# Another order of loads, products and conversions in an attention and two-MoE kernel

## The chip, the cores and the metric

The kernel runs on one core of a Trainium2 chip. The metric is device time in microseconds (us) of one execution; lower is better. A core has five engines with a queue of instructions each: TensorE (PE in the rows; its weight loads are PEld), VectorE (DVE), ScalarE (ACT), GpSimd (POOL) and SyncE (SP). SP issues most transfers; 16 DMA engines carry them. A row that names an engine with a q (SPq, PEldq) is about its sequencer.

## The reference

```python
def reference(**kwargs):
    attn_out = _attn_ref(q, k, v, f)             # b=4, h=8, s=576, d=64
    x = attn_out.transpose(0, 2, 1, 3).reshape(2304, 512)
    x = _moe_ref(x, w_in, w_out)
    return _moe2_ref(x, w_gate, w_output_gate, w1, w2)

def _attn_ref(q, k, v, f):
    cum = np.cumsum(np.log(np.clip(f, 0.0001, 1.0)), axis=-1)
    scores = q @ k.T / sqrt(64) + cum[:, None] - cum[None, :]   # causal, then softmax, then @ v

def _moe_ref(x, w_in, w_out):                    # (2304, 512), w_in (512, 2048), w_out (2048, 512)
    h = x @ w_in
    return (h * np.clip(h + 3.0, 0.0, 6.0) / 6.0) @ w_out

def _moe2_ref(x, w_gate, w_output_gate, w1, w2): # 8 experts, w1 (512, 1024), w2 (1024, 512) each
    e_idx = np.argmax(x @ w_gate, axis=1)        # one expert per token, softmax weight gate_w
    out[mask] = gate_w[mask, None] * eom[mask, e, None] * (np.maximum(x[mask] @ w1[e], 0.0) @ w2[e])
```

Here eom is a sigmoid of x @ w_output_gate. w_in and w_out are float64, the other inputs float32. The kernel splits each operand into a float16 part and a bfloat16 rest and forms each product as three products of the parts.

## The kernel before, in words

**Attention.** Tokens of a batch come in pieces: q and k of piece 0 to 3 (four heads by 256 positions) and 4 (the last 64 positions), v in blocks of 128. `load` issues a piece's loads on SP; `prep` splits a piece into its parts (`split_kq`: ScalarE, then GpSimd) and turns it by a transposing transfer of SP (tiles K and q); pieces 0 and 1 of batch 0 are turned by TensorE instead. `prep_v` splits a block of v. A unit is a head with one or two blocks of rows. `score` gives it its products (L349) and VectorE's reduce with the mask (L394), `soft` ScalarE's exponentials, `turn` or a transposing transfer the turned probabilities, `pv` the products with v. The list `plan` says in which order units ("q", "t") and preparations ("p", "v") come; `attn_seq` walks it. The first 16 units (`first_units`, batch 0) run before any chunk.

**First MoE.** Its 2304 tokens are cut into six chunks of 384. The first half of a chunk has 16 groups of 12 products 128x384 (L840, tile mm); ScalarE and VectorE make g of them (L848 to L855). The second half has 4 groups of 48 products (L867), which ScalarE and VectorE evict into x (L876, L877). A chunk is 32 parts, and between parts attention units are put in, as many as `goals` and the pace (PACE, and PACE_END from chunk 4 on) ask for: the units of a chunk are to be through by that share of its parts. w_in and w_out come raw (512-KB loads, tiles wo and raw), and VectorE and ScalarE make float32 of their bits (L793 to L809) at the steps that PRE_CONV and CONV_AT list.

**Gate and second MoE.** When attention is through, `open_weights` reuses its memory for the experts' weights: a ring of three 512-KB buffers (stw) that SP loads, ScalarE converts (L1040) and VectorE gives the rest of (L1043); one such step is put in at every second part of a chunk. `gate_steps` picks a token's expert and rank. `gather` fetches an expert's tokens by an indirect transfer of GpSimd and turns them by one of SP, `expert1` and `expert2` hold the two products (L1152, L1171), and GpSimd scatters the rows to the output (L1178). Tokens beyond 384 of an expert would take further rounds, behind an If on `more` at the end; a block beyond an expert's count stands in an If of its own. The counts are loaded into registers of every engine (L1409).

TensorE, ScalarE and VectorE take their work in the written order, and SP and GpSimd too in the start.

Of the kernel before, what the change touches and what calls it, by code (L numbers as in the profile page):

```python
# [23 lines left out]

ATTN_FIRST = 200

PACE, PACE_END = 0.82, 0.75

PRE_CONV = (1, 3, 5, 7, 9, 11, 13, 15, 17, 19, 21, 22, 28, 29, 29, 30)

CONV_AT = (3, 4, 5, 7, 9, 11, 12, 14, 16, 17, 19, 20, 22, 24, 25, 27)

# [26 lines left out]
def attention_moe_kernel(ctx: ExitStack, tc: tile.TileContext, q, k, v, f, w_in, w_out,  # L59
# [316 lines left out]
    def score(u):  # L376
        kind, b = u[0], u[1]
        if kind == "q":
            h, qbs = u[2], u[3]
            N = sum(QW[x] for x in qbs)  # L380
            ms = ap1.tile([P, 576], F32, tag="ms", name="ms", bufs=3)
            nm = ap1.tile([P, 4], F32, tag="nm", name="nm", bufs=4)
            offs, off = [], 0
            sc = ps_sc.tile([P, 512], F32, tag="sc", name="sc")
            for qb in qbs:
                l1, l2 = q_cols(b, h, qb)
                w = QW[qb]
                scores(sc[:, off:off + w], h, qb, l1, l2)
                off += w
            off = 0  # L390
            for i, qb in enumerate(qbs):
                w = QW[qb]
                ps = sc[:, off:off + w]
                nc.vector.tensor_tensor_reduce(  # L394
                    out=pairs(ms[:, off:off + w]), in0=ps[:, 0:w].rearrange("p (c j) -> p c j", c=2),
                    in1=pairs(mask[:, 640 - w:640]), scale=-1.0 / PSC, scalar=3e38, op0=ALU.add, op1=ALU.min,
                    accum_out=nm[:, i:i + 1])
                tick()
                offs.append((off, w, i))
                off += w  # L400
            st[u] = [ms, nm, offs, N]
        else:
            h = u[2] * 2
            N = 576
            ms = ap1.tile([P, 576], F32, tag="ms", name="ms", bufs=3)
            nm = ap1.tile([P, 4], F32, tag="nm", name="nm", bufs=4)
            for j, (c0, w) in enumerate(((0, 512), (512, 64))):
                ps = ps_sc.tile([P, 512], F32, tag="sc", name="sc")
                for e in range(2):
                    po = slice(e * 64, e * 64 + 64)  # L410
                    l1, l2 = q_cols(b, h + e, 4)
# [12 lines left out]
                tick()  # L424
            st[u] = [ms, nm, [(0, 576, 1)], N]
# [188 lines left out]
    for b in range(B):  # L614
# [3 lines left out]
        for hp in range(H // 2):  # L618
            gb += [("q", b, 2 * hp, (3,)), ("q", b, 2 * hp + 1, (3,)), ("t", b, hp)]
        if b == 0:  # L620
            plan += ga[0:2] + [("p", 0, 2)] + ga[2:5] + [("p", 0, 3), ga[5], ("v", 0, 2)] + ga[6:]
            ends.append(len(plan) - 1)
            plan += gc[0:3] + [("p", 0, 4)] + gc[3:6] + [("v", 0, 3)] + gc[6:] + [None, gb[0], None, gb[1], ("v", 0, 4)]
            ends.append(len(plan) - 1)
# [37 lines left out]
    def attn_seq():  # L662
# [36 lines left out]
        for i in range(2):  # L699
            load(i, "kq")  # L700
        load(0, "v")
        setup()
        store_decay(cp)
        for hh in range(2):
# [7 lines left out]
            behind.pop(0)()  # L712
        load_next(nc.scalar)
        load_next(nc.scalar)
        load(2, "kqv")
        yield "end"
        prep_v(0, 0)
        yield "end"
        prep_v(0, 1)
        yield "end"  # L720
        load(3, "kq")
        for it in plan:
# [273 lines left out]

    ring, made, fetches = [], [], []

    def weights_steps(wp):

        parts, tiles = [], {}

# [31 lines left out]
        for i, (_, e, which, js) in enumerate(parts):  # L1034
            if (e, which) not in tiles:
                tiles[e, which] = (wp.tile([P, 2, KD, F2], F16, tag="W1", name="W1", bufs=2) if which == 0 else
                                   wp.tile([P, 2, F2 // P, DM], F16, tag="W2", name="W2", bufs=2))
# [79 lines left out]
    def gather(e, blocks, into=None):  # L1117
# [5 lines left out]
        else:  # L1123
            xs, xg = into[0], [into[1]]
        for j, s in enumerate(blocks):
            nc.gpsimd.indirect_dma_start(out=xg[j], out_offset=None,  # L1126
                                         in_=rows[0:NT if into is None else NBL * P, :],
                                         in_offset=bass.IndirectOffsetOnAxis(ap=slot[s][0][:, e:e + 1], axis=0))
            nc.sync.dma_start_transpose(out=xs[:, :, j * P:(j + 1) * P], in_=xg[j])
            xs_t[e, s] = (xs, j * P)  # L1130

    def h_tile(e, blocks, into=None):
        if into is None:
            n = F2 // P * 2 * NSB * P
            into = wof[:, e % 2 * n:(e % 2 + 1) * n].rearrange("p (a c b) -> p a c b", c=2, b=NSB * P)
        for j, s in enumerate(blocks):
            h_t[e, s] = (into, j * P)

# [117 lines left out]
    def pre_step():  # L1256
# [3 lines left out]
        for _ in range(PRE_CONV.count(nsteps[0])):  # L1260
            convert()
        for _ in range(1 + ready):
            if loads and (loads[0][0] == "wi" or ready):
                load_next(nc.sync)

    with tc.manual_schedule(engines={mybir.EngineType.SP, mybir.EngineType.Pool}):
        while len(complete) < need[0]:
            pre_step()
        for _ in range(LEAD):
            pre_step()  # L1270
    gate.append(gate[-1])
    held = False
    EARLY_CONV_DONE = 2 * NF - len(conv)
    assert len(conv) == len(CONV_AT), (len(conv), nsteps)
    goals = [due[need[c + 1] - 1] for c in range(NCH - 1)]
    mp2 = None
    px_ctx = ctx.enter_context(ExitStack())
    iota = None
# [123 lines left out]
        fetches[0]()  # L1402
    for g_ in first:
        run(g_, F2 // P)
    for e in range(2):
        for _ in expert2(e, ps_mm, (0,), wi[:, 1, e, 0:2 * DM].bitcast(F32)):
            pass
        if e == 0:
            regs.extend(nc.values_load(cnt[0:1, x:x + 1], min_val=0, max_val=NT) for x in range(E))  # L1409
            more = nc.values_load(nrounds[0:1, 0:1], min_val=0, max_val=NT // CAP)  # L1410

    def round_(first):

# [11 lines left out]
        blocks = main  # L1425
        if not first:
            blocks = [(0, 1)] * E
            wg = weights_steps(wp)
# [16 lines left out]
    round_(True)  # L1445
    manual.close()
    with tc.If(more > 0):
        RA = wi.rearrange("p a b c -> p (a b c)")[:, 0:NB * CAP].rearrange("p (n s) -> p n s", s=CAP)
        with tc.For_i(0, more, 1):
            nc.vector.tensor_scalar(out=rank, in0=rank, scalar1=-float(CAP), scalar2=None, op0=ALU.add)  # L1450
            for i in range(NB):
                rank_onehot(RA, i, 0, CAP)
            table(RA, 0, mp2, ps_mm, range(NSB), NB)
            round_(False)


# [28 lines left out]
```

## Time and profile before

| | us |
|---|---|
| median of 3 runs (lowest, highest) | 830.68 (830.33, 832.77) |
| the profiled execution | 827.96 |
| its span, first to last instruction | 826.2 |
| TensorE busy in it | 731.0 (88%) |
| VectorE, ScalarE, GpSimd busy | 453.1, 454.8, 316.7 |

Each execution's time includes what lies around the span. The granted clock is TensorE's, as a share of 2.4 GHz; 0.50 is 1.2 GHz. Its mean over the span is 0.943. A wait is shown in square brackets behind an instruction: how long its engine stood idle ahead of it, and what came last before it started.

### The profile page before, as it was taken

How to read it: one execution, taken by the hardware profiler on the slowest of the kernel's cores; microseconds unless marked ns; L12 is line 12 of the kernel's file. 1: busy time of each engine (PE TensorE's matmuls, PEld its weight loads, DVE VectorE, ACT ScalarE, POOL GpSimd, SP SyncE). 2: the span in 40 equal slices, each digit the busy share in tenths (PEclk: the TensorE clock that was granted, in tenths of full speed). 3: DMA queues.
4: the chain of work that ended last, by engine and by line, in shares of the span. 5: the costliest groups of instructions: out<-in, count | busy, mean ns of one | idle time of the engine just before them, and what ended most of it. 6: DMA issues, size and time to landing. Idle time of an engine off the chain costs nothing. (4 is left out here: it accounts for less than half of the span.)

```text
span 826.2 us, 16592 instructions
## 1 busy us (share of the span) xinstructions
PE 731.0 (88%) x6153; PEld 477.5 (58%) x6153; DVE 453.1 (55%) x1254; ACT 454.8 (55%) x904; POOL 316.7 (38%) x402
## 2 busy tenths in 40 slices
PE   4366888699999989999799999889998999999994
PEld 2254455456566656666466566446676766756761
DVE  7587786556852574278434855683142565536420
ACT  4575678666874677278755772562022565545420
POOL 7485557584554434155543451000032222320010
PEclk7576998989999999999899999999999999999997
DMA  6996869986678646386765564863087789969100
GB/s 158 276 227 148 190 130 192 212 196 150 95 161 157 135 90 122 54 178 129 158 112 123 86 94 126 269 200 102 1 173 135 202 269 298 305 196 267 66 37 28
DMA packets 268066, 129.00 MB, mean 156 GB/s; under 512 B 218946, under 2 KB 251810, under 8 KB 267972
## 3 DMA queue, kind: packets, MB, share of 16 engines
q1 hardware_dynamic: 255620, 104.71, 59.0%
q0 software_dynamic: 4960, 15.73, 5.3%
q10 hardware_dynamic: 7392, 7.34, 2.9%
q8 instruction: 54, 0.88, 0.5%
q14 instruction: 40, 0.33, 0.1%
HBM read 71.52 MB, written 10.08 MB: 99 GB/s over the span
## 5 line engine op out<-in xcount | busy, mean ns | idle before, releaser
L867 PE MATMUL mm<-g,wo 128*128 128x384 f16 (+1 forms) x1152 | 197.5, 330 | 0.0
L840 PE MATMUL mm<-xT,wi 128*128 128x384 f16 x912 | 165.9, 338 | 7.3 <-DVE g L855 4.5
L840 PEld LDWEIGHTS <-wi 128*128 128x128 f16 (+1 forms) x1152 | 112.3, 100 | 83.3 <-issue 19.6
L867 PEld LDWEIGHTS <-wo 128*128 128x128 f16 (+1 forms) x1152 | 111.6, 99 | 71.9 <-issue 3.7
L465 POOL TENSOR_TENSOR pn<-ms,pn 128x384 bf16<-128x384 f32 (+1 forms) x80 | 80.9, 1013 | 85.9 <-ACT pn L464 53.7
L1152 PEld LDWEIGHTS <-W 128*128 128x128 f16 (+1 forms) x1344 | 99.9, 98 | 12.6 <-issue 4.2
L1152 PE MATMUL mm<-g,W 128*128 128x256 f16 (+3 forms) x1152 | 97.3, 246 | 3.3 <-issue 1.9
L1171 PE MATMUL mm<-W,wo 128*128 128x512 f16 (+1 forms) x432 | 94.5, 379 | 0.6 <-PEq L1436 0.5
L456 ACT ACTIVATE ms<-ms,nm 128x512 f32<-128x512 f32 (+3 forms) x144 | 80.3, 577 | 10.4 <-DVE nm L394 7.6
L1043 DVE TENSOR_TENSOR W<-stw,W 128x1024 bf16<-128x1024 f32 x46 | 55.7, 1223 | 52.4 <-ACT W L1040 51.6
L394 DVE CUSTOM_DVE_ANT_1 ms<-sc,mask 128x128 f32<-128x128 f32 (+3 forms) x128 | 60.6, 486 | 31.4 <-PE sc L349 25.5
L1171 PEld LDWEIGHTS <-wo 128*128 128x128 f16 (+1 forms) x432 | 41.8, 98 | 50.7 <-ACT W L1040 1.2
L1178 POOL DMA_INDIRECT out_dram<-wo,ids x18 | 20.6, 1145 | 124.3 <-ACT wo L1177 102.3
L877 DVE SCALAR_TENSOR_TENSOR x<-mm,x 128x384 bf16<-128x384 f32 x24 | 13.4, 557 | 98.5 <-ACT x L876 98.5
L876 ACT ACTIVATE x<-mm 128x384 f16<-128x384 f32 x24 | 11.7, 489 | 87.7 <-PE mm L867 86.9
L1156 DVE SCALAR_TENSOR_TENSOR wo<-mm,wo 128x128 bf16<-128x128 f32 (+1 forms) x96 | 33.0, 355 | 47.5 <-ACT wo L1155 44.1
L349 PE MATMUL sc<-K,q 128*128 128x128 f16 (+2 forms) x192 | 49.0, 312 | 10.7 <-DVE nm L394 5.7
L349 PE MATMUL sc<-K,Q 67*128 67x128 f16 (+2 forms) x192 | 48.7, 310 | 9.4 <-DMA K<-cumd 3.5
L848 ACT ACTIVATE hr<-mm,bias 128x384 f32<-128x384 f32 x76 | 43.7, 575 | 24.2 <-PE mm L840 24.0
L1040 ACT ACTIVATE W<-stw 128x1024 f16<-128x1024 f32 x46 | 47.7, 1050 | 16.7 <-DMA stw<-in_moe_w_dram 16.5
L849 DVE SCALAR_TENSOR_TENSOR mm<-hr,mm 128x384 f32<-128x384 f32 x76 | 42.4, 558 | 25.7 <-ACT hr L848 25.3
L501 PE MATMUL pv<-vt,pt 128*128 128x65 f16 x320 | 41.3, 198 | 17.1 <-ACT pt L450 11.0
(216 smaller groups left out, 1254.5 us busy)
## 6 DMA issues: line engine op xcount, KB each, us to landing
stw<-in_moe_w_dram SPq DMA_DIRECT2D x46, 512.0 KB
stx<-in_moe_w_dram SPq DMA_DIRECT2D x18, 512.0 KB
wo<-in_moe_w_in_dram SPq DMA_DIRECT2D x14, 512.0 KB
raw<-in_moe_w_out_dram ACTq DMA_DIRECT2D x10, 512.0 KB
rows<-rw POOLq DMA_DIRECT2D x15, 256.0 KB
ld<-in_v_dram SPq DMA_DIRECT2D x13, 256.0 KB
ld<-in_k_dram SPq DMA_DIRECT2D x12, 256.0 KB
ld<-in_q_dram SPq DMA_DIRECT2D x12, 256.0 KB
```

What stands on the lines that cost most here:

```text
L349: nc.tensor.matmul(po, lhsT=lhs[0:rows], rhs=r if n > 1 else r[:, :, 0], start=x == 0, stop=x == 1)
L394: nc.vector.tensor_tensor_reduce(out=pairs(ms[:, off:off + w]), in0=ps[:, 0:w].rearrange("p (c j) -> p c j", c=2), in1=pairs(mask[:, 640 - ...
L456: nc.scalar.activation(out=ms[:, off:off + w], in_=ms[:, off:off + w], func=AF.Exp, scale=-1.0, bias=nm[:, i:i + 1])
L465: nc.gpsimd.tensor_tensor(out=lo.bitcast(BF16), in0=ms[:, 0:N], in1=hi, op=ALU.subtract)
L840: nc.tensor.matmul(ps[:, 0:w], lhsT=l.bitcast(BF16) if a else l, rhs=r.bitcast(BF16) if b2 else r, start=i == 0, stop=i == 3 * KD - 1)
L848: nc.scalar.activation(out=hr, in_=pw, func=AF.Relu, bias=bias3)
L849: nc.vector.scalar_tensor_tensor(out=pw, in0=hr, scalar=6.0, in1=pw, op0=ALU.min, op1=ALU.mult)
L867: nc.tensor.matmul(ps[:, 0:w], lhsT=l.bitcast(BF16) if a else l, rhs=r.bitcast(BF16) if b2 else r, start=i == 0, stop=i == 3 * NF - 1)
L1040: nc.scalar.activation(out=hi, in_=sts[i], func=AF.Copy)
L1043: nc.vector.tensor_tensor(out=lo.bitcast(BF16), in0=st, in1=hi, op=ALU.subtract)
L1152: nc.tensor.matmul(ps[:, 0:w], lhsT=l.bitcast(BF16) if a else l, rhs=r.bitcast(BF16) if b2 else r, start=i == 0, stop=i == 3 * KD - 1)
L1171: nc.tensor.matmul(ps, lhsT=l.bitcast(BF16) if a else l, rhs=r.bitcast(BF16) if b2 else r, start=i == 0, stop=i == 3 * NF2 - 1)
```

## The change

Seven things are changed.

1. k and q of piece 2 are loaded right behind v's first block, and `prep(0, 2)` stands ahead of the first units; `plan` loses that step, and the last four entries of PRE_CONV come down by one.
2. `pre_step` issues a w_in load only when its conversion is due within RAW_AHEAD steps.
3. `fill` gives TensorE 10 products 128x128 of constant tiles into unused columns behind each first unit's scores, and 24 at the end of the start. Nobody reads them.
4. `goals` are raised by AHEAD in chunks 1 to 3, and PACE_END falls from 0.75 to 0.42.
5. Register loads of the counts: two at first, then one after each expert.
6. The seventh to the twelfth gather are issued behind the sixth.
7. The last block of the last expert comes behind the If of the further rounds, which gets memory of its own.

```diff
-PACE, PACE_END = 0.82, 0.75
-PRE_CONV = (1, 3, 5, 7, 9, 11, 13, 15, 17, 19, 21, 22, 28, 29, 29, 30)
+PACE, PACE_END = 0.82, 0.42
+PRE_CONV = (1, 3, 5, 7, 9, 11, 13, 15, 17, 19, 21, 22, 27, 28, 28, 29)
+AHEAD = (0, 3, 9, 9, 0)
+RAW_AHEAD = 7
+FILL, LAST_FILL = 10, 24
...
+    def fill(ps, n):
+        for _ in range(n):
+            nc.tensor.matmul(ps[:, 384:512], lhsT=minus, rhs=mask[:, 0:P], start=True, stop=True,
+                             skip_group_check=True)
...
+            if first_units(u):
+                fill(sc, FILL)
...
-            plan += ga[0:2] + [("p", 0, 2)] + ga[2:5] + [("p", 0, 3), ga[5], ("v", 0, 2)] + ga[6:]
+            plan += ga[0:2] + [("v", 0, 2)] + ga[2:4] + [("p", 0, 3)] + ga[4:]
...
         load(0, "v")
+        load(2, "kq")
         setup()
         store_decay(cp)
...
-        load(2, "kqv")
+        load(2, "v")
         yield "end"
         prep_v(0, 0)
+        prep(0, 2, "k")
         yield "end"
         prep_v(0, 1)
+        prep(0, 2, "q")
...
         for _ in range(1 + ready):
-            if loads and (loads[0][0] == "wi" or ready):
+            ahead = 2 * NF - len(loads) < sum(x <= nsteps[0] + RAW_AHEAD for x in PRE_CONV)
+            if loads and (ready or loads[0][0] == "wi" and ahead):
                 load_next(nc.sync)
...
         for _ in range(LEAD):
             pre_step()
+        fill(cur["o"], LAST_FILL)
...
-    goals = [due[need[c + 1] - 1] for c in range(NCH - 1)]
+    goals = [due[need[c + 1] - 1] + x for c, x in enumerate(AHEAD)]
...
+            with tc.issue_after(gathered[5]) if 6 <= len(gathered) < 12 else nullcontext():
+                t = nc.gpsimd.indirect_dma_start(
...
+    def load_counts(n):
+        for x in range(len(regs), len(regs) + n):
+            src = cnt[0:1, x:x + 1] if x < E else nrounds[0:1, 0:1]
+            regs.append(nc.values_load(src, min_val=0, max_val=NT if x < E else NT // CAP))
...
-            regs.extend(nc.values_load(cnt[0:1, x:x + 1], min_val=0, max_val=NT) for x in range(E))
-            more = nc.values_load(nrounds[0:1, 0:1], min_val=0, max_val=NT // CAP)
+            load_counts(2)
...
-            spread(expert2(e, ps2, blocks[e]), F2 // P // 2 * len(blocks[e]), n2)
+            bl = blocks[e] if e < E - 1 or not first else blocks[e][:-1]
+            if first and e < E - 1:
+                load_counts(1)
+            spread(expert2(e, ps2, bl), F2 // P // 2 * len(bl), n2)
...
     round_(True)
...
     manual.close()
-    with tc.If(more > 0):
...
+    further_rounds()
...
+    for _ in expert2(E - 1, ps2, main[E - 1][-1:]):
+        pass
```

On SP, in the start, from the second block of v on, before (tile wo holds raw w_in; the transposes of K and q in the ninth and tenth row are those of piece 2):

```order
L191 DMA g<-in_v_dram 128x8x64
L196 DMA g<-in_k_dram 128x4x128
L196 DMA g<-in_q_dram 128x4x128
L191 DMA g<-in_v_dram 128x8x64
L777 DMA wo<-in_moe_w_in_dram 128x4x256 x3
L196 DMA g<-in_k_dram 128x4x128
L196 DMA g<-in_q_dram 128x4x128
L777 DMA wo<-in_moe_w_in_dram 128x4x256 x3
L296 DMA_TRANSPOSE K_94<-kp 128x8x128
L321 DMA_TRANSPOSE q_289<-qp 128x8x64 x2
L777 DMA wo<-in_moe_w_in_dram 128x4x256 x3
```

The same place of the changed kernel, from the first block of v on:

```order
L197 DMA g<-in_v_dram 128x8x64
L202 DMA g<-in_k_dram 128x4x128
L202 DMA g<-in_q_dram 128x4x128
L155 DMA cumd<-cp 32x15x128
L217 DMA K_95<-cumd 3x4x512 x2
L197 DMA g<-in_v_dram 128x8x64 x2
L794 DMA wo<-in_moe_w_in_dram 128x4x256 x3
L202 DMA g<-in_k_dram 128x4x128
L202 DMA g<-in_q_dram 128x4x128
L308 DMA_TRANSPOSE K_94<-kp 128x8x128
L333 DMA_TRANSPOSE q_254<-qp 128x8x64 x2
L794 DMA wo<-in_moe_w_in_dram 128x4x256 x3
```

Piece 2's k and q now stand ahead of the decay store (cumd), and three w_in loads instead of six ahead of its transposes.

On ScalarE, from the last eviction but one of chunk 4's second half on, before (W<-stw is a weight conversion, x an eviction of the second half, hr and g belong to the first half of chunk 5):

```order
L876 ACTIVATE x_7013<-mm 128x3x128
L1040 ACTIVATE W_7182<-stw 128x1024
L1040 ACTIVATE W_7313<-stw 128x1024 x3
L876 ACTIVATE x_7013<-mm 128x3x128
L1040 ACTIVATE W_7313<-stw 128x1024
L848 ACTIVATE hr<-mm,bias_86 128x384
L1040 ACTIVATE W_7569<-stw 128x1024
L852 ACTIVATE g<-mm 128x384
L848 ACTIVATE hr<-mm,bias_86 128x384
L1040 ACTIVATE W_7569<-stw 128x1024
```

The second half of chunk 4 in the changed kernel, from its start to the first row of chunk 5:

```order
L1058 ACTIVATE W_7237<-stw 128x1024 x3
L893 ACTIVATE x_7296<-mm 128x3x128
L1058 ACTIVATE W_7237<-stw 128x1024
L1058 ACTIVATE W_7358<-stw 128x1024 x2
L893 ACTIVATE x_7296<-mm 128x3x128
L1058 ACTIVATE W_7358<-stw 128x1024 x2
L1058 ACTIVATE W_7477<-stw 128x1024 x3
L893 ACTIVATE x_7296<-mm 128x3x128
L1058 ACTIVATE W_7477<-stw 128x1024
L1058 ACTIVATE W_7718<-stw 128x1024 x4
L893 ACTIVATE x_7296<-mm 128x3x128
L865 ACTIVATE hr<-mm,bias_86 128x384
```

All 16 conversions now stand ahead of chunk 5's rows; before, the last nine came behind chunk 4's last eviction.

## Rows read from the trace of the kernel before

**Rows 1.** Windows chosen by hand, busy time, granted clock, DMA share and rate

```profile
core 0: us, PE busy (x) PEld busy (x) DVE busy (x) ACT busy (x) POOL busy (x), PEclk, DMA share, GB/s
7.50:13.50 6.00, 3.17 (x19) 2.23 (x17) 5.80 (x9) 2.73 (x6) 5.71 (x9) 0.86 0.10 23
14.00:37.70 23.70, 8.39 (x58) 6.03 (x58) 16.92 (x49) 8.46 (x19) 9.41 (x10) 0.57 1.13 264
76.40:80.10 3.70, 3.65 (x12) 1.72 (x12) 2.25 (x4) 0.00 (x0) 0.21 (x1) 0.50 0.98 291
187.10:521.30 334.20, 319.58 (x2796) 204.32 (x2795) 186.36 (x618) 211.62 (x435) 141.09 (x181) 0.99 0.64 125
```

**Rows 2.** Windows by stage: start, chunk 4's second half, chunk 5's halves

```profile
14.00:76.40 62.40, 30.66 (x276) 23.25 (x277) 46.07 (x133) 36.61 (x77) 41.45 (x56) 0.64 0.91 216
...
485.80:521.30 35.50, 35.50 (x283) 22.45 (x281) 17.92 (x62) 13.58 (x25) 8.06 (x13) 1.00 0.61 142
521.30:565.30 44.00, 36.77 (x251) 21.45 (x249) 33.13 (x76) 27.39 (x46) 1.65 (x3) 0.92 0.64 190
565.30:596.70 31.40, 31.40 (x203) 18.98 (x200) 3.90 (x15) 2.25 (x5) 2.02 (x2) 1.00 0.25 67
```

**Rows 3.** Timeline of SP's queue: start, length, instruction

```profile
14.80 0.58 SPq L196 DMA_DIRECT2D g<-in_k_dram  x1
...
23.91 4.22 SPq L777 DMA_DIRECT2D wo<-in_moe_w_in_dram  x3
28.23 3.34 SPq L296 DMA_TRANSPOSE K<-kp  x1
```

**Rows 4.** Timeline of ScalarE, the start

```profile
37.81 0.63 ACT L223 ACTIVATE kp<-g 128x512 f16<-128x512 f32 x1 [8.12 <-DMA K<-kp]
```

**Rows 5.** Timeline of TensorE, the start

```profile
18.39 0.31 PE L349 MATMUL sc<-K,q 128*128 128x128 f16 x1
18.50 0.31 PE L349 MATMUL sc<-K,Q 67*128 67x128 f16 x1
...
49.19 0.39 PE L349 MATMUL sc<-K,Q 67*128 67x256 f16 x1 [3.08 <-POOL Q L265]
```

**Rows 6.** TensorE's waits from 521.3 to 565.3: total, times, longest

```profile
PE mm L933 <- DVE g L855: 2.7, 1, 2.7
PE mm L840 <- DVE g L855: 2.6, 2, 1.5
PE mm L967 <- DVE ohsum L958: 2.0, 1, 2.0
```

**Rows 7.** Tile stw from 480 to 566: durations in ns, first and last start

```profile
L1040 ACT ACTIVATE W<-stw x16: 1053/1056/1058, 512.0 to 546.5; 128x1024 f16<-128x1024 f32 x16
L1043 DVE TENSOR_TENSOR W<-stw,W x16: 1212/1224/1226, 513.1 to 548.0; 128x1024 bf16<-128x1024 f32 x16
```

**Rows 8.** Line L394 from 52 to 66.5, VectorE's reduces

```profile
L394 DVE CUSTOM_DVE_ANT_1 ms<-sc,mask x7: 547/548/552, 52.2 to 66.2; 128x384 f32<-128x384 f32 x7
```

**Rows 9.** TensorE's waits from 565 to 640, and its rows of line L1409

```profile
PE mm L1152 <- issue: 1.9, 3, 1.0
PE mm L1152 <- DMA g<-g: 0.7, 1, 0.7
...
L1409 PEldq TENSOR_LOAD <-cnt x8: 300/306/490, 611.8 to 614.8; - x8
```

**Rows 10.** The end: ScalarE's timeline, and rows of lines L1447 and L1480

```profile
814.94 0.69 ACT L1177 ACTIVATE wo<-mm,cf 128x512 f32<-128x512 f32 x1 [4.49 <-PEq L1447]
...
L1447 POOLq EVENT_SEMAPHORE  x4: 17/43/2031, 816.5 to 816.8; - x4
...
L1447 PEldq COMPARE_BRANCH  x1: 3556/3556/3556, 810.8 to 810.8; - x1
...
L1447 POOLq INC_SWDGE_SEM  x1: 1401/1401/1401, 818.8 to 818.8; - x1
...
L1480 POOLq DRAIN  x3: 50/107/5133, 820.3 to 826.0; - x3
```

**Rows 11.** Timeline of VectorE, the start

```profile
25.18 0.69 DVE L793 TENSOR_SCALAR cv<-wo 128x512 int32<-128x512 int32 x1 [2.13 <-DMA wo<-in_moe_w_in_dram]
```

More of the change, by code (lines that the diff above doesn't have):

```diff
@@ L997, in attention_moe_kernel, with weights_steps @@
     ring, made, fetches = [], [], []
-    def weights_steps(wp):
+    def weights_steps(wp, room2=None):
         parts, tiles = [], {}
@@ L1036, in weights_steps @@
                 tiles[e, which] = (wp.tile([P, 2, KD, F2], F16, tag="W1", name="W1", bufs=2) if which == 0 else
-                                   wp.tile([P, 2, F2 // P, DM], F16, tag="W2", name="W2", bufs=2))
+                                   wp.tile([P, 2, F2 // P, DM], F16, tag="W2", name="W2", bufs=2) if room2 is None
+                                   else room2)
                 wts[e, which] = tiles[e, which]
@@ L1103, in attention_moe_kernel @@
     xs_t, h_t = {}, {}
+    hrooms = [2]
     def rank_onehot(R, i, s0, s1):
@@ L1109, in attention_moe_kernel @@
     taken = [0]
+    gathered = []
     def row_tile(room):
@@ L1125, in gather @@
         for j, s in enumerate(blocks):
-            nc.gpsimd.indirect_dma_start(out=xg[j], out_offset=None,
-                                         in_=rows[0:NT if into is None else NBL * P, :],
-                                         in_offset=bass.IndirectOffsetOnAxis(ap=slot[s][0][:, e:e + 1], axis=0))
+            with tc.issue_after(gathered[5]) if 6 <= len(gathered) < 12 else nullcontext():
+                t = nc.gpsimd.indirect_dma_start(
+                    out=xg[j], out_offset=None, in_=rows[0:NT if into is None else NBL * P, :],
+                    in_offset=bass.IndirectOffsetOnAxis(ap=slot[s][0][:, e:e + 1], axis=0))
+            gathered.append(t.ins)
             nc.sync.dma_start_transpose(out=xs[:, :, j * P:(j + 1) * P], in_=xg[j])
@@ L1134, in h_tile @@
             n = F2 // P * 2 * NSB * P
-            into = wof[:, e % 2 * n:(e % 2 + 1) * n].rearrange("p (a c b) -> p a c b", c=2, b=NSB * P)
+            into = wof[:, e % hrooms[0] * n:(e % hrooms[0] + 1) * n].rearrange("p (a c b) -> p a c b", c=2, b=NSB * P)
         for j, s in enumerate(blocks):
@@ L1427, in round_ @@
             blocks = [(0, 1)] * E
[L1428 removed]
+            wg = weights_steps(wp, wif[:, 8192:16384].rearrange("p (a b c) -> p a b c", a=2, c=DM))
             run(wg, 4 * KD + 1)
@@ L1442, in round_, with further_rounds @@
                 fetch(e + 2, (0, 1, 2))
-            spread(expert2(e, ps2, blocks[e]), F2 // P // 2 * len(blocks[e]), n2)
+            bl = blocks[e] if e < E - 1 or not first else blocks[e][:-1]
+            if first and e < E - 1:
+                load_counts(1)
+            spread(expert2(e, ps2, bl), F2 // P // 2 * len(bl), n2)
+    def further_rounds():
+        RA = wif[:, 0:NB * CAP].rearrange("p (n s) -> p n s", s=CAP)
+        hrooms[0] = 1
+        with tc.If(regs[E] > 0):
+            with tc.For_i(0, regs[E], 1):
+                nc.vector.tensor_scalar(out=rank, in0=rank, scalar1=-float(CAP), scalar2=None, op0=ALU.add)
+                for i in range(NB):
+                    rank_onehot(RA, i, 0, CAP)
+                table(RA, 0, mp2, ps_mm, range(NSB), NB)
+                round_(False)
+    wif = wi.rearrange("p a b c -> p (a b c)")
+    assert (E - 1) % 2 and NB * CAP <= 8192
     round_(True)
+    kept = [dict(x) for x in (wts, slot, h_t)]
     manual.close()
-    with tc.If(more > 0):
[L1448 to L1454, printed above, removed]
+    further_rounds()
+    for x, y in zip((wts, slot, h_t), kept):
+        x.update(y)
+    for _ in expert2(E - 1, ps2, main[E - 1][-1:]):
+        pass
 _INS = ["q", "k", "v", "f", "moe_w_in", "moe_w_out", "moe2_w_gate", "moe2_w_output_gate", "moe2_w1", "moe2_w2"]
```

## The prediction

> **What bounds the kernel now.** I read the view of windows by stage first, because the limits differ from stage to stage. In it TensorE is the engine to beat nearly everywhere: from 187.1 to 521.3 us it is busy for 319.58 of 334.2 us [rows 1], and the second half of the last chunk, 565.3 to 596.7, is full to the brim: 31.40 busy of 31.40, at a granted clock of 1.00 [rows 2]. Time can come only from the stretches where it isn't so. There are two long ones. From 14.0 to 76.4, before the first chunk, TensorE is busy for 30.66 of 62.40 us, and its granted clock is 0.64, a mean over stretches at either level (1.2 and 2.4 GHz) [rows 2]. The first half of the last chunk, 521.3 to 565.3, takes 44.00 us with 36.77 busy at a clock of 0.92 [rows 2], although it has as many 128x384 products of its own (192) as the second half, which needs 31.40.
>
> Then I read the queue of SP beside the timelines of ScalarE and TensorE for the start. SP issues the loads of k and q of piece 2 at 14.80, three w_in loads at 23.91 that occupy it for 4.22 us, and only at 28.23 the transpose of piece 2's K [rows 3]. ScalarE, next to need a buffer that this transpose reads, stands still for 8.12 us until 37.81 [rows 4]. The DMA engines move 264 GB/s from 14.0 to 37.7, but only 23 GB/s from 7.5 to 13.5 [rows 1]: the same bytes are late in one place and could have gone in another. Later TensorE waits 3.08 us for GpSimd's copy of Q [rows 5].
>
> For the last chunk I read TensorE's waits and the rows of tile stw. TensorE waits 2.7, 2.6 and 2.0 us, each time on VectorE [rows 6]. VectorE there has rests of weight conversions in between (L1043, 1224 ns each, 16 of them from 513.1 to 548.0) [rows 7]: they stand in its order ahead of what TensorE needs.
>
> **The change part by part.** All terms are against the profiled execution: 827.96 us, with a span of 826.2, so 1.76 lie around it. It lies 2.7 us below the median of the runs, 830.68; I add these 2.7 at the end.
>
> *Start: piece 2 in front, w_in by need.* k and q of piece 2 (0.52 MB) go ahead of the decay store, into the stretch that moves 23 GB/s. Three w_in loads (1.57 MB) go behind the transposes. So 2.1 MB less are ahead of the transpose, at 264 GB/s [rows 1] 7.9 us. ScalarE's wait of 8.12 us can give that. Against it: prep of piece 2 now stands before the first units and the units behind it come one place earlier, so one unit less covers the wait. Seven units start their reduce from 52.2 to 66.2 [rows 8], 2.3 us apart: −2.3. GpSimd's copies for piece 2 are also asked for earlier, so the wait of 3.08 us should go: +3.1. Bounds: nothing, if another transfer takes the place of the w_in loads, to 12, where the wait for the transpose, the copy and the clock term below all go.
>
> *Products without use.* 184 products of 128 columns are added, 10 behind each of 16 first units' scores and 24 at the end. Starts of such a product lie 0.11 us apart at half clock (18.39 to 18.50) [rows 5]: 1.1 us a unit, half of it at full clock. At 2.3 us a unit there is room for 0.55 beside what TensorE does (30.66 of 62.40), hardly for 1.1; VectorE's reduce stands behind them by the count that it waits for. I take −1.5, a unit or two at half clock; bounds 0 and −17.6 (16 units at 1.1). What they buy: the first chunk's first 3.7 us are granted 0.50 [rows 1]; at full clock half of them go, +1.8. The start in all: 7.9 − 2.3 + 3.1 − 1.5 + 1.8 = 9.0.
>
> *Attention sooner (AHEAD, PACE_END).* Its last products leave the second half of chunk 4 and are spread over chunks 1 to 4. The columns stay the same, so only the 14.6 us idle there (334.2 less 319.58 [rows 1]) can change. I take +2, a seventh of them: more units early also means fuller queues on VectorE and GpSimd. Bounds +6 and −8 (the next step twice).
>
> *Conversions leave the last chunk.* All 16 now stand in the second half of chunk 4. At ScalarE they ran from 512.0 to 546.5 [rows 7], 35.5 us with the last one's 1.06; the new place offers 31.4 to 35.5 us [rows 2], so at worst they end 4 us behind it. Weighed against that, 512-KB loads are what set their pace, and SP now issues them with no gate's transposes in between. I cost it at nothing beyond the bound above; the cover is the loads' lead of three buffers, and without it ScalarE's first eviction of chunk 5 stands behind the last conversion. What it brings: the first half of chunk 5 loses most of its 7.2 us idle (44.00 less 36.77) and of the half clock that follows such waits. A mean clock of 0.92 over 44.0 us is 7.0 us at half level, 3.5 lost [rows 2]. I leave 1.2 for the gate's own chain (the third wait [rows 6]): 7.2 + 3.5 − 1.2 = 9.5. Bounds 5 (half the waits stay) and 10.7.
>
> *Gathers in order, register loads.* TensorE waits 0.7 us on the gather's transfer and 1.9 on issue after the last chunk [rows 9]; its queue has 8 count loads of 306 ns in a row there, 2.4 us [rows 9]. Two now, then one per expert, hidden behind queued products. +1.2; bounds 0 and 2.6.
>
> *Last block after the If.* The last scatter is today followed by a wait of up to 2.03 us and a 1.40 us counter update of the If's end [rows 10], then by GpSimd's drain of 5.13 [rows 10]. The first two now come one block earlier, beside 24 products. The drain stays. +2.0; bounds +3.4 (both), and −1, if TensorE runs dry between the If and the last products.
>
> TensorE's branch of this If took 3.56 us at 810.8, while its queued products ran on; ScalarE's last eviction starts at 814.94 [rows 10]. I cost its new place at nothing, since again about 4 us of products are queued ahead of it. The Trainium skill, "Runtime: NRT & Kernel Launch", section "Instruction fetch mechanics", says that a taken branch to a page outside the sequencer's window must fetch that page before anything goes on, which speaks against putting work behind a branch. The trace agrees that the branch is long, but not that products stop for it. By the rule this term would be 2.0 − 3.6 = −1.6; by the row it is 2.0.
>
> **Sum:** 9.0 + 2.0 + 9.5 + 1.2 + 2.0 = 23.7. 827.96 − 23.7 = 804.3 for a profiled execution, 807.0 as median.
>
> **The rivals.** *R1, the useless products eat the start.* If reduces wait for them at half clock in more units, at 1.1 us each, eight units cancel the 9.0: 816. For it: the clock is 0.64 there [rows 2] and VectorE's reduce starts each unit's chain. Against: the products themselves fill TensorE, which was half idle.
>
> *R2, the conversions spill out of chunk 4.* ScalarE's hr of chunk 5 waits 4 us for the last of them and VectorE's rests follow at 1.2 us: with the middle at −6 instead of +2, 815. For it: 35.5 us of conversions against 31.4. Against: pace was also lost to other work in between.
>
> *R3, more than I count.* Start at 12, middle at +6: 807.0 − 3 − 4 = 800.
>
> *R4, slower: w_in by need comes late.* Eleven of SP's w_in loads now stand behind the transposes. VectorE waited 2.13 us once for such a load [rows 11]. If the start is bound by w_in's transfers, the 7.9 us are lost as well, and with each of the eleven late by 2.13 the kernel takes 807.0 + 7.9 + 23.4 = 838.3; it is slower than before from eight such waits on ((23.7 − 7.9)/2.13 = 7.4). Against: eight of the eleven stood behind the transposes before too, and one wait is all that they show.
>
> *R5, the branch in front of the last block stops TensorE.* 3.56 us more than I count: 810.6. For it: nothing of the block can be queued before the branch is decided. Against: the products queued today outlasted it [rows 10].
>
> **How the numbers follow.** Forecast 0.52 (802 to 812 if its small terms vary within their bounds), R1 0.15, R2 0.09, R3 0.10, R5 0.10, R4 0.04. The likeliest case gives 807.0. The range 797 to 820 takes in R1, R2, R3 and R5; outside are R4 and the far ends. A measurement of this kernel tells about 0.3% (2.5 us) from no change: only R4 and a sum of R1 and R2 at their worst reach 828, so faster 0.93, same 0.04, slower 0.03.
>
> **What would show it.** Right: ScalarE's wait ahead of piece 2's split ends near 30 us, not 37.81; the first chunk starts 9 us sooner at a clock near 1; no conversion stands in the first half of the last chunk and that half takes 34 to 35 us; the second half of chunk 4 near 31.4; from the last eviction to the end 2 us less. Wrong: reduces in the start that wait for TensorE (R1); waits on stw that hold up chunk 5's first products (R2); VectorE's raw steps waiting for wo<-in_moe_w_in_dram (R4); TensorE idle for 3 us ahead of the last 24 products (R5).

## The result, and the profile after

The changed kernel takes 823.97 us in the median of six runs (822.73 to 826.05), the kernel before 830.57 in the same six rounds: a ratio of 0.9914, 95% interval 0.9894 to 0.9934. It is faster by 0.9%, about 7 us; 23.7 were forecast, and the forecast's range ended at 820, below the fastest run. The profiled execution was the slowest of the six, 826.05 us with a span of 824.3. So I read a second profile beside it: e1 is the same kernel in a later round, 819.29 us in its profiled execution, where 827.96 is that of before.

The table holds the lengths of the stages, each from the first product of one stage to that of the next in the traces; the experts end with TensorE's last product.

| stage | before | changed | e1, changed again | forecast gain | gain in e1 |
|---|---|---|---|---|---|
| to the first chunk | 76.5 | 70.8 | 69.2 | 9.0 | 7.3 |
| chunk 0 | 110.6 | 111.6 | 109.6 | (in the start) | 1.0 |
| chunks 1 to 4 | 334.3 | 343.1 | 341.5 | 2.0 | −7.2 |
| chunk 5, first half | 44.0 | 40.3 | 38.4 | 9.5 | 5.6 |
| chunk 5, second half | 31.2 | 31.2 | 31.2 | 0 | 0 |
| experts | 218.3 | 219.3 | 219.6 | 1.2 | −1.3 |
| behind the last product | 11.4 | 8.0 | 8.0 | 2.0 | 3.4 |

But for rounding the last column adds up to 8.67, which is 827.96 − 819.29, so the stages leave nothing out. Not all of it is the change: in e1's round the kernel before took 825.12 in the median, not 830.57, and e1's ratio of 0.993 stands for 5.8 us. A profile shows one execution, so a stage is read below from all profiles that share its settings. Two of the five terms have the wrong sign.

The view of windows by stage of the changed kernel, first profile (start, chunk 1's first half, chunk 4's second half, chunk 5's first half; columns as in [rows 1]):

```profile
14.00:70.80 56.80, 39.50 (x461) 33.78 (x462) 48.38 (x136) 36.92 (x77) 41.83 (x56) 0.80 1.01 232
182.40:239.90 57.50, 50.44 (x459) 31.14 (x458) 38.78 (x121) 40.42 (x82) 26.62 (x33) 0.89 0.74 129
...
494.30:525.50 31.20, 31.20 (x193) 18.78 (x193) 21.10 (x43) 14.99 (x19) 0.46 (x1) 1.00 0.71 229
525.50:565.70 40.20, 35.02 (x251) 20.86 (x250) 26.80 (x70) 21.48 (x39) 1.65 (x3) 0.92 0.43 119
```

The start answers to [rows 2]: the granted clock rose from 0.64 to 0.80 and the stage is 5.6 us shorter. The second row is where the time went. Chunk 1's first half is 57.5 us long with 7.1 idle and a clock of 0.89; the same stage of the kernel before, in the same view:

```profile
187.10:234.70 47.60, 45.03 (x439) 28.63 (x438) 35.72 (x108) 36.30 (x76) 23.70 (x29) 1.00 0.68 130
```

It has 20 products fewer there, 2.6 us idle and the full clock. Chunk 4's second half came out as forecast (31.20), but chunk 5's first half still holds 5.2 us idle, at a clock of 0.92 as before. That wait has another cause than those of [rows 6]. TensorE's waits from 525.5 to 565.7, and below them ScalarE's timeline of that place:

```profile
PE mm L857 <- DVE x L894: 5.2, 1, 5.2
```

```profile
523.98 0.47 ACT L893 ACTIVATE x<-mm 128x384 f16<-128x384 f32 x1
525.03 1.06 ACT L1058 ACTIVATE W<-stw 128x1024 f16<-128x1024 f32 x1 [0.58 <-DMA stw<-in_moe_w_dram]
526.34 1.06 ACT L1058 ACTIVATE W<-stw 128x1024 f16<-128x1024 f32 x1 [0.25 <-DMA stw<-in_moe_w_dram]
528.85 1.06 ACT L1058 ACTIVATE W<-stw 128x1024 f16<-128x1024 f32 x1 [1.45 <-DMA stw<-in_moe_w_dram]
531.57 1.06 ACT L1058 ACTIVATE W<-stw 128x1024 f16<-128x1024 f32 x1 [1.67 <-DMA stw<-in_moe_w_dram]
533.66 1.06 ACT L1058 ACTIVATE W<-stw 128x1024 f16<-128x1024 f32 x1 [1.03 <-DMA stw<-in_moe_w_dram]
534.62 0.47 ACT L893 ACTIVATE x<-mm 128x384 f16<-128x384 f32 x1
```

Five conversions stand ahead of chunk 4's last eviction, each waits for its load, and the eviction starts at 534.62, nine us after chunk 4's last product. VectorE's part of it follows, and TensorE, which needs that accumulator back, waits 5.2 us.

In the experts the wait for the gather and those on issue [rows 9] are gone, and a new one stands in their place. TensorE's waits from 597 to 825:

```profile
PE mm L1193 <- ACT W L1058: 2.7, 1, 2.7
PE mm L1174 <- DVE wo L1178: 1.6, 2, 1.1
PE mm L1193 <- ACTq L1466: 1.0, 2, 0.5
```

The end: timelines of TensorE and GpSimd, and the sequencer rows of the If (L1482) and of the program's end (L1525), which answer to [rows 10]:

```profile
805.43 5.34 PE L1193 MATMUL mm<-W,wo 128*128 128x512 f16 x24
810.92 5.34 PE L1193 MATMUL mm<-W,wo 128*128 128x512 f16 x23
...
817.31 0.99 POOL L1200 DMA_INDIRECT out_dram<-wo,ids  x1 [4.50 <-ACT wo L1199]
...
L1482 PEldq COMPARE_BRANCH  x1: 3766/3766/3766, 806.7 to 806.7; - x1
...
L1482 POOLq INC_SWDGE_SEM  x1: 1381/1381/1381, 814.7 to 814.7; - x1
...
L1525 POOLq DRAIN  x3: 50/113/6362, 817.1 to 824.0; - x3
```

The counter update now lies at 814.7, ahead of the last scatter; the drain follows that scatter directly.

### The profile page after: what moved, and what is told of

Same layout as the page of the kernel before. It is cut to its first block, busy times and chain, and to the rows that moved or that the text cites. A ratio compares the mean times of both kernels' runs of the same rounds, so it can differ in the third digit from the quotient of the medians.

```text
span 824.3 us, 16955 instructions
## 1 busy us (share of the span) xinstructions
PE 740.9 (90%) x6326; PEld 488.8 (59%) x6337; DVE 454.0 (55%) x1254; ACT 455.1 (55%) x904; POOL 316.4 (38%) x402
## 5 line engine op out<-in xcount | busy, mean ns | idle before, releaser
L865 ACT ACTIVATE hr<-mm,bias 128x384 f32<-128x384 f32 x76 | 43.8, 577 | 31.3 <-PE mm L857 31.2
L361 PE MATMUL sc<-K,q 128*128 128x128 f16 (+2 forms) x192 | 47.6, 306 | 11.4 <-DVE nm L408 5.8
L872 DVE TENSOR_TENSOR g<-mm,g 128x384 bf16<-128x384 f32 x76 | 42.1, 556 | 22.6 <-ACT g L869 21.9
L1177 ACT ACTIVATE wo<-mm 128x128 f16<-128x128 f32 (+1 forms) x96 | 31.1, 331 | 41.3 <-PE mm L1174 34.7
```

Of the source, the lines that this page charges most:

```text
L361: nc.tensor.matmul(po, lhsT=lhs[0:rows], rhs=r if n > 1 else r[:, :, 0], start=x == 0, stop=x == 1)
L865: nc.scalar.activation(out=hr, in_=pw, func=AF.Relu, bias=bias3)
```

## The experiments

Twelve kernels: the changed one again, and eleven edits of it. Ratios are to the kernel before on the same chip, with their 95% intervals; its median went from 825.1 to 829.6 us between the rounds of the experiments, so times in us of different rounds are not compared.

**e1, the changed kernel again.** No edit.

> The changed kernel once more, for a second profile. Theory A (the units drawn into chunk 1 make its first half wait and drop the clock): the first half of chunk 1 again takes over 54 us (57.5 in the first profile, 47.5 before). Theory B (that stretch was an accident of one execution): it takes 48 to 50 here, and the time lost is found elsewhere. Time 823 to 825 in either case.

Measured: 0.993 (0.9898 to 0.9961), 819.44 us in the median. Chunk 1's first half takes 56.4 us: theory A's number, not an accident. TensorE's waits there:

```profile
PE pv L513 <- DMA pt<-pn: 2.5, 1, 2.5
PE sc L361 <- DVE nm L435: 2.2, 1, 2.2
PE sc L429 <- DVE nm L408: 1.2, 1, 1.2
```

Windows of that half and of chunks 1 to 4:

```profile
178.80:235.20 56.40, 49.99 (x460) 31.02 (x458) 38.72 (x121) 40.39 (x82) 26.59 (x33) 0.91 0.73 130
178.80:520.30 341.50, 321.27 (x2797) 204.46 (x2795) 194.61 (x626) 217.99 (x443) 140.63 (x181) 0.99 0.69 133
```

The waits are those of attention units: scores that wait for VectorE's reduce of the unit ahead, and products with v that wait for the turned probabilities. The granted clock of this stage is 0.91 here and 0.89 in the first profile.

**e2, the old pace.**

```diff
-PACE, PACE_END = 0.82, 0.42
-AHEAD = (0, 3, 9, 9, 0)
+PACE, PACE_END = 0.82, 0.75
+AHEAD = (0, 0, 0, 0, 0)
```

> AHEAD all 0 and PACE_END 0.75, as before; all else as changed. Theory A: chunks 1 to 4 return from 343 to about 334 us and chunk 5's first half from 40 to 44, so the time is 824 - 9 + 4 = 819. Theory B: chunks 1 to 4 stay as long as they are, and only chunk 5 loses its 4 us: 828.

Measured: 0.9932 (0.9903 to 0.9962), as e1 on the same chip. Its windows of chunk 1's first half, chunks 1 to 4, chunk 4's second half and chunk 5's first half:

```profile
183.10:230.90 47.80, 45.05 (x438) 28.59 (x437) 35.91 (x108) 36.29 (x76) 23.69 (x29) 1.00 0.78 132
183.10:518.10 335.00, 320.16 (x2797) 204.21 (x2796) 187.54 (x619) 212.78 (x435) 141.12 (x181) 0.99 0.69 125
482.60:518.10 35.50, 35.50 (x283) 22.36 (x281) 18.67 (x63) 14.02 (x25) 8.12 (x13) 1.00 0.56 143
518.10:562.50 44.40, 37.06 (x252) 21.46 (x251) 32.30 (x76) 26.97 (x45) 1.64 (x3) 0.92 0.59 187
```

Both halves of theory A's mechanism show: chunks 1 to 4 return to 335.0, chunk 5's first half to 44.4. Its sum doesn't: 6.5 us gained and 6.0 lost against e1 is nothing. Attention sooner is worth nothing in this kernel as it is. The halves say where the 6.5 us go: against e2, e1 loses 8.5 in chunk 1's first half and 7.7 in the second halves of chunks 2 and 3, and gains 8.2 in chunk 3's first half and 4.2 in chunk 4's second; the rest lies in the first halves of chunks 2 and 4. The crowded half of chunk 3 was moved to chunk 1, not removed.

**e3, the written order to the end of chunk 5.** The close of the manual schedule moves from `open_weights` to the end of the chunk loop.

```diff
-        wlo = None
-        main.close()
         px_ctx.close()
...
     run(wg_, 4 * KD + 1 - nw)
+    for lo in wlo:
+        lo()
+    wlo = None
+    main.close()
```

> ScalarE, VectorE and TensorE keep the written order through chunks 4 and 5, so that eight conversions stand in chunk 4's second half and eight between the rows of chunk 5. Theory A (the conversions all ahead of chunk 4's last eviction wait for their loads and hold chunk 5 up): the wait of 5.2 us and the half clock behind it go, chunk 5's first half takes 34 to 36 instead of 40, time 819. Rival (conversions beside chunk 5's rows cost what they did before): 42 to 44 us, time 827.

Measured: 1.0023 (0.9993 to 1.0053), slower than the changed kernel by 1%. The rival's number, but not quite its reason: the wait for the last eviction did go, and others came at the far end of the stage. TensorE's waits from 523.5 to 569:

```profile
PE mm L1102 <- DVE R L1125: 3.2, 2, 2.2
PE mm L857 <- DVE g L872: 3.2, 2, 1.9
PE mm L1102 <- DVE g L872: 1.5, 1, 1.5
```

VectorE's ranking work (R, L1125) in written order now holds up TensorE. The edit changed more than the conversions, and so can't price them; e7 does.

**e4, no products without use.**

```diff
-FILL, LAST_FILL = 10, 24
+FILL, LAST_FILL = 0, 0
```

> FILL and LAST_FILL 0: the 184 products whose result nobody reads are left out, nothing else. If they buy clock and cost little: the granted clock from 14 to 70 falls from 0.80 to about 0.65, the first chunk starts 1 to 3 us later, time 826. If they delay the reduces (rival R1): the first chunk starts 2 us or more earlier, time 822.

Measured: 0.9896 (0.9856 to 0.9936). The windows up to the first chunk and of its first 3.7 us:

```profile
14.00:67.50 53.50, 30.25 (x277) 22.86 (x278) 47.60 (x135) 36.60 (x77) 41.79 (x56) 0.70 0.98 246
67.50:71.20 3.70, 3.70 (x12) 1.68 (x12) 0.79 (x2) 0.00 (x0) 0.00 (x0) 0.50 1.12 331
```

Both effects are there. The clock is lower, 0.70 and then 0.50 as in [rows 1], and still the first chunk starts at 67.5, where all eight profiles with ten products a unit have it start at 68.4 to 70.9. Its interval overlaps that of e1, so the time doesn't decide between the forecasts.

**e5, w_in as early as its room allows.**

```diff
-RAW_AHEAD = 7
+RAW_AHEAD = 99
```

> RAW_AHEAD 99: w_in loads are issued as early as their room allows, as before; piece 2 stays in front. If w_in by need brings the transposes forward (1.57 MB at 264 GB/s): the transpose of piece 2's K lands 5 to 6 us later, the first chunk starts at 74 to 76 instead of 69 to 71, ratio to the kernel before 0.999. Rival (the early loads of piece 2 alone do it): the first chunk starts within 1 us of 70, ratio 0.993.

Measured: 0.9912 (0.9882 to 0.9941), the first chunk at 68.4. ScalarE's wait for the transpose and SP's issue of it:

```profile
30.11 0.63 ACT L229 ACTIVATE kp<-g 128x512 f16<-128x512 f32 x1 [2.10 <-DMA K<-kp]
```

```profile
15.37 4.56 SPq L794 DMA_DIRECT2D wo<-in_moe_w_in_dram  x3
...
21.53 4.13 SPq L308 DMA_TRANSPOSE K<-kp  x1
```

The rival holds. Even so, only three w_in loads stand ahead of piece 2's transpose: preparing piece 2 ahead of the first units already put the other three behind it. The condition on w_in moves nothing that counts.

**e6, chunk 1's goal as before.**

```diff
-AHEAD = (0, 3, 9, 9, 0)
+AHEAD = (0, 0, 9, 9, 0)
```

> AHEAD (0, 0, 9, 9, 0): chunk 1 gets only the units it had before. Theory A (a first half that is given more than some 52 score products waits and loses the clock): chunk 1's first half takes 48 instead of 56 to 57 us, chunk 2 takes the three steps for at most 3 us more, ratio 0.986. Rival (the waits follow the units): chunk 2's first half grows past 52 us and the ratio stays 0.993.

Measured: 0.9922 (0.9905 to 0.9939). Windows of chunk 1's and chunk 2's first halves:

```profile
181.10:229.00 47.90, 45.06 (x439) 28.61 (x438) 35.99 (x109) 36.37 (x76) 23.74 (x29) 1.00 0.74 132
266.10:316.70 50.60, 45.21 (x418) 28.94 (x417) 33.21 (x108) 40.76 (x88) 25.45 (x33) 0.93 0.73 136
```

Chunk 1 loses its 9 us, as theory A says; chunk 2's first half takes 50.6 instead of e1's 45.7. Chunks 1 to 4 come to 338.6, 2.9 less than in e1, where theory A wanted 5 or more. Neither the ratio nor the profile can tell that from nothing: the eight profiles with AHEAD (0, 3, 9, 9, 0) have 340.1 to 345.5 there, e10 and e12 with e6's goal 343.1 and 339.4. Part of the waits followed the units, as the rival says, though its 52 us were not reached.

**e7, conversions between the evictions.** As e3, but the written order ends with chunk 4, and from its 21st part on each part gets a conversion.

```diff
+            for lo in wlo:
+                lo()
+            wlo = None
+            main.close()
             R = wp.tile([P, NB, CAP - P], F16, name="R")
...
-            if wg_ and k_ > 1 and k_ % 2 == 0 and nw < 4 * KD + 1:
+            if wg_ and k_ > 1 and (k_ % 2 == 0 or c == NCH - 2 and k_ > 20) and nw < 4 * KD + 1:
```

> The written order is kept on ScalarE, VectorE and TensorE until chunk 4 ends, with a conversion at every part from the 21st on, so that all but two conversions lie between chunk 4's evictions and none waits ahead of the last one in a row of five; chunk 5 is scheduled as in the changed kernel. Theory A (conversions that wait for their loads in front of chunk 4's last eviction cost chunk 5 a wait of 4 to 5 us and the clock): chunk 5's first half takes 35 to 36 us instead of 38 to 40, ratio 0.988. Rival (the loads' pace is what costs, wherever the conversions stand): chunk 4's second half grows from 31 to 34 or more, ratio 0.993.

Measured: 0.988 (0.9857 to 0.9904). Its windows of chunk 4's second half and chunk 5's first half, and TensorE's waits in the latter:

```profile
492.60:524.70 32.10, 31.39 (x194) 18.78 (x192) 21.86 (x44) 15.26 (x19) 0.46 (x1) 1.00 0.67 216
524.70:562.50 37.80, 35.00 (x253) 20.86 (x251) 26.27 (x69) 20.86 (x38) 1.65 (x3) 0.95 0.47 127
```

```profile
PE mm L950 <- DVE g L872: 1.9, 1, 1.9
PE mm L857 <- DVE g L872: 0.5, 1, 0.5
PE mm L857 <- DVE x L894: 0.3, 1, 0.3
```

The wait for the last eviction falls from 4 to 5 us to 0.3: theory A's mechanism is shown. That eviction still stands behind four conversions in a row, but it starts at 528.49, 3.8 us after chunk 4's last product and not 8 to 9. Its size was off, since a wait of the gate's products takes 1.9 back and chunk 4 pays 0.9: both halves take 69.9 us in this profile, 71.5 in the first of the changed kernel and 69.6 in e1. So the profile, of the slowest of its four executions (823.97 us), shows no gain in sum. The ratio is better, but its interval overlaps that of the changed kernel: a gain in time is not shown.

**e8, all counts at once.**

```diff
-            load_counts(2)
+            load_counts(E + 1)
...
-            if first and e < E - 1:
-                load_counts(1)
```

> All nine register loads of the counts at once, as before; none between the experts. If the count load behind the If is what TensorE waits for 2.7 us near 691 to 700 us: that wait goes, with the half clock behind it, and the wait of some 2 us at the first experts returns; the experts take 203 to 205 us instead of 206, ratio 0.991. Rival (the If itself stops TensorE there): the wait of 2.7 stays and the register loads come on top, ratio 0.995.

Measured: 0.9906 (0.9876 to 0.9937). The experts take 216.7 us from the end of the chunks to the last product instead of e1's 219.6, and no wait of theirs is longer than 0.5:

```profile
PE mm L1174 <- issue: 0.5, 2, 0.3
PE mm L1174 <- DVE wo L1178: 0.5, 1, 0.5
PE mm L1193 <- issue: 0.5, 1, 0.5
```

The wait of 2.7 is gone, against the rival, though e2, e9 and e12, with the loads in place, lack it too; the wait of some 2 us at the first experts, which the first forecast wanted back, didn't come. The profile puts the wait of 2.7 down to a ScalarE conversion, but that is not what ended it: in e6 the conversion ends at 690.67, while TensorE goes on at 691.24, when a count load on its sequencer, begun at 690.35, is through. The sequencer's rows there, branch of the If and count load, in e1 (with the wait) and in e2 (without):

```profile
L1466 PEldq COMPARE_BRANCH  x1: 227/227/227, 686.7 to 686.7; - x1
...
L1434 PEldq TENSOR_LOAD <-cnt x1: 626/626/626, 690.9 to 690.9; - x1
```

```profile
L1466 PEldq COMPARE_BRANCH  x1: 2138/2138/2138, 690.5 to 690.5; - x1
...
L1434 PEldq TENSOR_LOAD <-cnt x1: 312/312/312, 692.8 to 692.8; - x1
```

In e1 the sequencer shows nothing for 1.8 us ahead of the load, and then the load takes 0.63. In e2 the branch itself took 2.14, beside products that were already queued, and the load followed at once.

**e9, twice the products without use.**

```diff
-FILL, LAST_FILL = 10, 24
+FILL, LAST_FILL = 20, 24
```

> FILL 20 instead of 10, so 344 products whose result nobody reads. If they delay the reduces (what e4 suggests, a start of 67.5 us without them against 68.4 to 70.9 with ten): the first chunk starts 2 to 3 us later still, at 72 or after, ratio 0.996. Rival (e4's early start was an accident of one execution and the products cost nothing): 69 to 71 us with a clock near 1.00 before the first chunk, ratio 0.992.

Measured: 0.9891 (0.9857 to 0.9926). The first chunk starts at 71.2, later than in any profile with ten, at a clock of 0.91 before it and 1.00 after:

```profile
14.00:71.20 57.20, 43.20 (x620) 38.99 (x621) 48.21 (x136) 36.92 (x77) 41.87 (x56) 0.91 1.00 231
71.20:74.90 3.70, 3.68 (x22) 2.14 (x22) 1.27 (x3) 1.50 (x3) 0.00 (x0) 1.00 1.14 331
```

So the products do delay the start, by less than forecast for twenty (72 or after). That chunk 0 gives a part back isn't shown: it takes 108.6 us here, 108.3 to 112.9 in the four profiles without products and 109.2 to 112.2 in the eight with ten. None, ten and twenty can't be told apart in the time.

**e10, combined.** The edits of e4, e6, e7 and e8 together.

```diff
-AHEAD = (0, 3, 9, 9, 0)
+AHEAD = (0, 0, 9, 9, 0)
...
-FILL, LAST_FILL = 10, 24
+FILL, LAST_FILL = 0, 0
...
-            load_counts(2)
+            load_counts(E + 1)
```

> The changed kernel without the 184 products whose result nobody reads, with all counts loaded at once, chunk 1's goal as before and the conversions spread as in e7. If what the single runs showed adds up (0.3% each for products and counts, 0.5% for the conversions, 0.1% for the goal, from 0.992): ratio 0.980 to 0.982. Rival (the same waits and clock drops return elsewhere): 0.986 or more.

Measured: 0.9827 (0.9784 to 0.987), 816.03 us, between the two forecasts; the interval takes in both. Chunk 5's first half takes 36.6 at a clock of 1.00; but TensorE waits 4.9 us in one piece behind the nine count loads:

```profile
PE mm L1193 <- issue: 5.3, 2, 4.9
```

**e11, combined at the old pace.** The edits of e2, e4 and e8.

```diff
-PACE, PACE_END = 0.82, 0.42
+PACE, PACE_END = 0.82, 0.75
...
-AHEAD = (0, 3, 9, 9, 0)
+AHEAD = (0, 0, 0, 0, 0)
...
-FILL, LAST_FILL = 10, 24
+FILL, LAST_FILL = 0, 0
...
-            load_counts(2)
+            load_counts(E + 1)
...
-            if first and e < E - 1:
-                load_counts(1)
```

> As e2 (AHEAD all 0, PACE_END 0.75), without the 184 products and with all counts at once, conversions scheduled as in the changed kernel. If attention sooner is worth nothing in all, 0.993 - 0.003 - 0.003 = 0.987, behind e10 by what the spread conversions bring. Rival (its early units were the main loss): as fast as e10, 0.981.

Measured: 0.9859 (0.9811 to 0.9906), near the first number, with an interval that overlaps e10's. Chunks 1 to 4 and chunk 5's first half take 334.4 and 44.3 us here, 343.1 and 36.6 in e10: 378.7 against 379.7.

**e12, e10 with counts expert by expert.** Against e10:

```diff
-            load_counts(E + 1)
+            load_counts(2)
...
+            if first and e < E - 1:
+                load_counts(1)
```

> e10 with the counts loaded as in the changed kernel, two at first and one after each expert. If nine loads in a row are what TensorE waits 4.9 us for in e10, and the single ones cost a wait of about 2.7 behind one expert's If: the first goes and the second comes back, last product 2 to 3 us earlier than in e10's profile, ratio 0.980. Rival (the waits of the experts are an accident of one execution, not of the loads' place): neither pattern returns and the ratio stays 0.983.

Measured: 0.9816 (0.978 to 0.9853), 813.02 us, the lowest ratio here, though its interval overlaps those of e10 and e11. It beats the kernel before by 1.8%, and its interval lies below that of the changed kernel (0.9894 to 0.9934), with which it shared no round. The wait of 4.9 is gone, as forecast; that of 2.7 did not come back. Neither pattern returned, as the rival has it, and the ratio can't decide between 0.980 and 0.983.

## Why the prediction was wrong, point by point

**The step that failed is the third, attention sooner: "only the 14.6 us idle there (334.2 less 319.58 [rows 1]) can change", and "I take +2".** It took the idle time of chunks 1 to 4 as something that units put there earlier would fill. The runs show the opposite: with AHEAD (0, 3, 9, 9, 0) these chunks take 340.1 to 345.5 us in eight profiles, with the old goals and pace 334.3 to 335.0 in three (before, e2, e11), with the same number of products (2797 in e1 and e2). So the term is −7.2 in e1 where +2 was forecast. In e1 TensorE is idle for 20.2 us in these chunks (341.5 less 321.3 busy) instead of 14.6, and in chunk 1 the granted clock falls at those waits. A first half with 438 products runs in 47.8 us at the full clock, with 460 in 56.4. The count alone doesn't decide: in e6 chunk 2's first half waits 5.4 us with 418. The windows by half chunk of the kernel before held the warning; its chunk 3, first half:

```profile
349.80:404.50 54.70, 47.96 (x448) 30.87 (x447) 37.28 (x126) 40.90 (x86) 27.49 (x34) 0.94 0.76 155
```

At 448 products it waited for 6.7 us. I read the four chunks as one window. The bound of −8 was about right, but by luck: I had taken it from the conversions' step, not from units. That chunk 1's goal sets where these waits fall is shown by e6; that goals and pace cost chunks 1 to 4 about what they save in chunk 5 is shown by e2 (379.4 us for both together, e1 379.9), and e11 beside e10 fits it.

**Conversions leave the last chunk: +9.5 forecast, 3.7 and 5.6 measured.** Direction and place were right. Their new place, of which I wrote "I cost it at nothing beyond the bound above", is rival R2, and it came in its own form: the loads' pace (16 conversions from 501.1 to 533.7, as slow as in [rows 7]) holds up chunk 4's last eviction, which the order rows showed five conversions behind the one before. e7 takes this wait away. The ring of three buffers, which I had counted as cover, is a part of that pace: SP could issue the next load only when VectorE had formed the rest of a conversion and so given its buffer back. SP's longest wait in e1 from 488 to 532:

```profile
SPq L1044 <- DVE W L1061: 27.0, 16, 3.1
```

What is left of the stage without this wait, 36.5 to 38.9 us in e7, e10 and e12, shows that 34.5 was too low in any case: the gate's products (line 950; line 933 in [rows 6]) wait 1.9, 2.4 and 2.7 us there, where I left 1.2 for the whole chain, and TensorE is busy for 33.3 to 35.1.

**Start: 9.0 forecast, 5.7 and 7.3 measured.** The first term was right in size: ScalarE's wait ends at 30.1 in e1 and e5 instead of 37.81, 7.7 us earlier for 7.9 forecast. But I put 1.57 MB of it down to w_in by need, and e5 shows that the moved preparation does it alone. The terms of the start but for the products without use come to 8.7, and the four profiles without these products show it: the first chunk starts at 67.3 to 68.0, 8.5 to 9.1 earlier than before. That the sum fits doesn't price its parts, of which only the first was tested by itself; TensorE's wait for GpSimd's copy of Q is in no profile after. With ten products a unit the first chunk starts at 68.4 to 70.9, 2.5 later in the mean, where I took 1.5, and at 71.2 with twenty. The +1.8 for the clock didn't show: the first 3.7 us of the chunk are granted 1.00 in e9 and in four of the eight profiles with ten (e1, e3, e5, e8), but 0.50 to 0.57 in the other four, and chunk 0 is no shorter than without. R1 is right in mechanism and wrong in price.

**Experts: +1.2 forecast, −1.3 measured.** The gathers in order did take their wait away; it is in no profile after. The register loads, forecast to be "hidden behind queued products", are not: with one load behind each expert, six profiles show a wait of 2.5 to 2.8 us near 690 to 700 (e4 one of 1.5), and e8, e10 and e11, with all at once, show none there. But e2, e9 and e12, with the single loads, show none either. In the six, TensorE's sequencer shows nothing for 1.5 to 1.9 us ahead of the load, the load takes 0.56 to 0.93, and the branch of the If before it took 0.21 to 0.23; in the other seven the branch took 0.33 to 2.28 and no such pause follows. What brings the pause stays open.

For nine loads in a row the cover decides: they took 4.5 us in e8, 5.1 in e11 and 6.0 in e10, and products queued ahead ran beside them for 4.0, 1.5 and 1.1, which left TensorE idle for 0.5, 3.6 and 4.9. In the kernel before the same nine, from 611.8 to 615.6, stopped TensorE for 0.14 us only. So I misread [rows 9]: the 1.9 on issue lie at 625.6 to 628.0, and the loads had cost next to nothing.

**Last block after the If: +2.0 forecast, 3.4 measured,** at the upper bound: from ScalarE's last eviction (816.35) to the end of the span it is 7.9 us instead of 11.3 [rows 10], about the update's 1.40 and the wait of 2.03 together. R5 falls: TensorE's branch took 3.77 us at 806.7, and its products stopped for 0.15 (5.34 us of them from 805.43, the next at 810.92), and in the other profiles no longer, except for 0.56 in e4. The rule of the Trainium skill on taken branches ("Runtime: NRT & Kernel Launch", section "Instruction fetch mechanics") fits the long branch, though no run shows that a fetch made it long; queued products covered it.

R3 and R4 didn't come. The sum of the terms as measured in e1 is 8.7; chunks 1 to 4 alone are 9.2 below their forecast, chunk 5 is 3.9 below, the experts 2.5, the start with chunk 0 0.7, and the end 1.4 above. That is the 15 us between 23.7 and 8.7.

## What to carry to other kernels

Work that is moved out of a crowded stage has to be priced in the stage that takes it, by that stage's own slack on every engine; a mean over several stages hides the one that is full. Where a scheduler may place conversions that wait for loads, look at what stands behind them on their engine: here an eviction, and with it TensorE. And undo the parts one by one: of seven edits, two (piece 2 in front, the block behind the If) show their gain in every profile, one, attention sooner, cancelled itself out, two (products without use, w_in by need) did nothing that the times could show, and two met in the experts and gave about nothing together.

## What the runs showed of the hardware

A count's register load on TensorE's queue took 0.30 us at best, but up to 1.07 in e10 and 1.30 in e1; nine in a row cost TensorE between 0.14 us (before) and 4.9 (e10) of idle time. A branch of its sequencer of 3.5 to 4.0 us, at the last If, let queued products run on. Waits of TensorE of 2 us or more often went with a stretch at half clock, in chunks 0, 1 and 5, and in the experts behind four of the six waits of 2.5 to 2.8 (691.9 to 695.3 in e1) and behind those of 4.9 and 3.6. Such a wait then costs more than its length: some 1.7 us more in e1, an estimate from 3.4 us at half the clock.
